# A routed mixture of experts behind an attention block on one Trainium2 core: eight blocks' P2 and P4 held back to the end of the last group

## The chip, the cores and the metric

The kernel runs on one core of one Trainium2 chip. The metric is device time in microseconds for one execution, taken as the median of several; lower is better. A profiled execution also gives the span from the first to the last instruction, the granted TensorE clock and one record for every instruction. PE is TensorE (PEld its weight loads), DVE is VectorE, ACT is ScalarE, POOL is GpSimd, SP is SyncE, which here only issues DMAs.

## The reference

An attention block with sketched features gives x with N = 4352 rows and 128 columns. Its second half routes x through eight experts:

```
logits = x @ w_gate
P = np.exp(logits - logits.max())
for _ in range(8):
    P /= P.sum(1, keepdims=True) + 1e-09
    P /= P.sum(0, keepdims=True) + 1e-09
    P *= N / E
for e in range(E):
    h = np.maximum(x @ w1[e], 0.0)      # 1024 columns
    out += P[:, e:e + 1] * (h @ w2[e])
```

All data is float32. The eight experts' two products for all rows are nearly all of the work. The routing weights are not negative, so P may be multiplied into x ahead of the ReLU.

## The kernel before

**Groups and blocks.** Rows stand transposed in `xT` (128 features by 4352 rows). They are cut into groups (line 529). Groups of two tiles come first with experts 0 and 1, without weights, while attention and routing still run; their sums are kept in `kept`. Then come five groups of three tiles with weighted rows, and at the end one last group: rows 0 to 511 as two tiles of 256, experts 2 to 7. Four blocks make up an expert there, 24 the group. A block is two of the eight slices of 128 hidden columns.

**The first product.** `first` (line 787) makes one step: two matmuls, one for each half of 64 columns of TensorE, into one of four PSUM banks named `a`, and a ReLU on ACT from there into `h`. A block has four steps, `h[0]` to `h[3]` (two slices by two tiles). The rows come weighted: `prepare_x` (line 569) loads the weights of expert e into `xe` by a DMA from `pT` on SP, and POOL multiplies `xT` into it. There are two `xe` buffers.

**The second product.** A 2x2 product of blocks is done with seven half-size products P1 to P7 instead of eight. They need differences of `h` (`ts`, made by DVE at lines 812, 814 and 815) and of w2 (`ws`). `seven` (line 870) says which product goes into which of four PSUM banks `s0` to `s3` and which half s of the 128 partitions of it (0 the lower, 1 the upper): P1 and P6 into `s0`, P2 and P4 into `s1`, P3 and P5 into `s2`, P7 into `s3`, in the half of the block's parity. Products run `LAG` = 8 steps, two blocks, behind the first product. Even blocks run half 0 ahead of half 1, odd blocks the other way, so that successive matmuls take the two halves in turn. `second` (line 921) counts products of each bank and half, and calls `part` when both halves of a bank have had their last.

**The order at the end.** `steps` issues a step of the first product, DVE's differences and the due products in turn. The order of each engine's queue comes from a scheduler; the attention and routing part fixes DVE's and PE's order by hand, the last part (lines 1060 and 1061) does not. `last_products` (line 888) gives the products of the last two blocks as P1 P6 P3 P5 P7, then P7 P1 P6 P3 P5, then the two blocks' P2 and P4. Bank `s3` completes first, then `s0`, `s2` and `s1`. `last_part` (line 660) evacuates them: ACT and DVE copy between halves of partitions, DVE adds the sums and the kept sums `k1` and `k2` of experts 0 and 1 (the two tiles of `kept[0]`) to the two results `y1` and `y2`, and `put` (line 599) transposes each and stores it in four DMAs, spread over the queues of line 751.

**The kept sums.** `weigh_kept` (line 583) loads the weights of experts 0 and 1 into `pb` by SP and lets POOL multiply both kept sums and add them. It is issued at the start of the group's fourth expert, expert 5 (line 960), behind the loads of the next expert on SP.

Of the kernel before, what the change touches and what calls it, by code (L numbers as in the profile page):

```python
# [13 lines left out]
Alu = mybir.AluOpType  # L14
# [36 lines left out]
def kernel(  # L51
# [12 lines left out]
    nc = tc.nc  # L64
# [457 lines left out]


    NMAX = 512
    NT3 = 256
# [57 lines left out]
    def weigh_kept(g):  # L583
# [6 lines left out]
        for y in ys[1:]:  # L590
            tc.keep_in_program_order(nc.gpsimd.tensor_tensor(ys[0], ys[0], y, op=Alu.add))

    lower, upper = slice(0, H2), slice(H2, P)

# [10 lines left out]
    def part(g, k):  # L605

        if groups[g][2] == 3:
            part_of_twenty(g, k)
        elif g == len(groups) - 1:
            last_part(g, k)  # L610
        else:
            part_of_seven(g, k)
# [46 lines left out]

    def last_part(g, k):  # L660

        lo, n, *_ = groups[g]
        s = sums[g][k]

        def add(out, a, b):
            nc.vector.tensor_tensor(out, a, b, op=Alu.add)

        own = parts.setdefault(g, {})
        if not own:
            own.update(y=[pools[0].tile([P, NT3], F32, name=f"y{t}", bufs=1)[:, 0:n] for t in range(2)],  # L670
                       **{a: room(a, n) for a in "zwxfr"})
        (y1, y2), z, w, x, f, r = (own[a] for a in "yzwxfr")
        k1, k2 = (kept[0][:, lo + t * n:lo + (t + 1) * n] for t in range(2))
        if k == 3:
            nc.scalar.copy(w[lower], k2[lower])
            nc.scalar.copy(r[upper], s[lower])
            add(w[upper], s[upper], r[upper])
            add(x[upper], w[upper], k1[upper])
            add(w[upper], w[upper], k2[upper])
        elif k == 0:  # L680
            nc.scalar.copy(z[lower], s[upper])
            nc.vector.tensor_copy(z[upper], s[lower])
            add(z, s, z)
            add(x[upper], x[upper], z[upper])
            add(x[lower], s[lower], k1[lower])
            add(z, z, w)
        elif k == 2:
            nc.scalar.copy(f[lower], s[upper])
            nc.scalar.copy(f[upper], s[upper])
            add(z[lower], s[lower], z[lower])  # L690
            add(y2, z, f)
            put(y2, lo + n, n, ends[1])
        else:
            add(y1, s, x)
            put(y1, lo, n, ends[0])

# [53 lines left out]

    ends = (nc.scalar, nc.sync, nc.gpsimd, nc.scalar), (nc.sync, nc.scalar, nc.gpsimd, nc.sync)

    def store(yt, b0, b1, queues):
# [13 lines left out]
    blocks = [(j, q) for j in range(len(items)) for q in range(FO // (4 if tiles_of(j) == 3 else 2))]  # L767
    LAG = 8
    hs = {}

    def room_of(k):

        lo, n, t, _, weighted = groups[items[blocks[k][0]][0]]
        if t == 3:
            if "x" not in hs:
                hs["x"] = pools[0].tile([P, 25, NT3], F32, name="hx", bufs=1)
                hs["pqg"] = pools[0].tile([P, 3, NT3], F32, name="pqg", bufs=1)
            return hs["x"] if k % 2 == 0 else hb[:, 0:25 * NT3].rearrange("p (b n) -> p b n", n=NT3)
        base = hs["x"].rearrange("p b n -> p (b n)") if weighted else hb
        size = 4 * (NT3 if weighted else 480)  # L780

        def at(i):
            return base[:, size * i:size * (i + 1)].rearrange("p (b n) -> p b n", b=4)[:, :, 0:n]

        return at(k % 3), at(3 + k % 2)

# [12 lines left out]
    def two(k):  # L799

        j, q = blocks[k]
        n = groups[items[j][0]][1]
        h, ts = hs[k] = room_of(k)

        def step(c):
            f, t = 2 * q + c // 2, c % 2
            first(k, f, t * n, (t + 1) * n, h[:, c], k % 2)

        def sums(c):

            if c == 4:
                nc.vector.tensor_tensor(ts[:, 0:2], h[:, 1::2], h[:, 0:2], op=Alu.subtract)  # L812
            elif c == 5:
                nc.vector.tensor_tensor(ts[:, 2], h[:, 3], ts[:, 0], op=Alu.subtract)  # L814
                nc.vector.tensor_tensor(ts[:, 3], h[:, 2], ts[:, 2], op=Alu.subtract)

        return 4, step, sums
# [52 lines left out]
    def seven(k):  # L870

        j, q = blocks[k]
        _, w2, ws = loaded_w[j]
        h, ts = hs[k]
        n = h.shape[2]
        lo, hi = slice(0, H2), slice(H2, DM)
        p1 = (w2[:, 2 * q, lo], h[:, 0], 0, 0, 0)
        p6 = (ws[:, 1, q], ts[:, 2], 0, 1, 0)
        p2 = (w2[:, 2 * q + 1, lo], h[:, 2], 1, 0, 0)
        p4 = (w2[:, 2 * q + 1, hi], ts[:, 3], 1, 1, 0)  # L880
        p3 = (ws[:, 3, q], h[:, 3], 2, 0, 0)
        p5 = (ws[:, 0, q], ts[:, 0], 2, 1, 0)
        p7 = (ws[:, 2, q], ts[:, 1], 3, k % 2, 0)
        if k % 2 == 0:
            return [p1, p6], [p2, p4], [p3, p5], [p7]
        return [p6, p1], [p4, p2], [p5, p3], [p7]

    def last_products(k):

        (p1, p6), (p2, p4), (p3, p5), (p7,) = seven(k)  # L890
        (r6, r1), (r4, r2), (r5, r3), (r7,) = seven(k + 1)
        ps = [(k, p) for p in (p1, p6, p3, p5, p7)] + [(k + 1, p) for p in (r7, r1, r6, r3, r5)] + [
            (k, p2), (k, p4), (k + 1, r2), (k + 1, r4)]
        return [ps[2 * i:2 * i + 2] for i in range(7)]

# [24 lines left out]

    def second(k, p):
        j, q = blocks[k]
        g, e = items[j]
        lo, n, t, es, _ = groups[g]
        w, x, i, s, place = p
        if g not in sums:
            sums[g] = [mps.tile([P, 512], F32, tag=f"s{i}", name="s")[:, 0:n * (t - 1)] for i in range(4)]
            done[g] = {}


        seen = done[g]
        c = seen[i, s] = seen.get((i, s), 0) + 1
        per = len(es) * (FO // (4 if t == 3 else 2)) * TIMES[t][i][s]
        if t == 2 and i == 3:
            per //= 2
        nc.tensor.matmul(sums[g][i][H2 * s:H2 * (s + 1), n * place:n * (place + 1)], w, x, start=c == 1,  # L936
                         stop=c == per, tile_position=(0, H2 * s))
        if c == per:
            seen[i] = seen.get(i, 0) + 1
            if seen[i] == 2:  # L940
                part(g, i)

    def steps():

        todo, sums_at, t = {}, {}, 0
        for k in range(len(blocks) + 2):
            if k == len(blocks):
                for i, ps in enumerate(last_products(k - 2)):
                    todo[t + i] = ps
            if k < len(blocks):  # L950
# [3 lines left out]
                if q == 0:  # L954
                    for i in (j, j + 1, j + 2 if j + 2 < first_weighted else j):
                        if i < len(items) and i not in sources and (pools or i < first_weighted):
                            prepare_x(i)
                        if i < len(items) and i not in loaded_w and (pools or i < first_weighted):
                            prepare_w(i)
                    if weighted and e == es[3]:  # L960
                        weigh_kept(g)
                m, step, sums_ = (four if tiles == 3 else two)(k)
                products = (twenty if tiles == 3 else seven)
# [37 lines left out]

    engines = mybir.EngineType
    with tc.manual_schedule(engines={engines.DVE, engines.PE, engines.Activation}):
# [88 lines left out]
```

## Time and profile before

| | |
|---|---|
| median of 3 timed runs | 948.29 us (947.58 to 948.32) |
| the profiled execution's own time | 947.29 us |
| its span, first to last instruction | 945.5 us |
| granted TensorE clock over the span | 0.997 |
| PE busy | 928.3 us (98%) |
| PE's weight loads busy | 548.7 us (58%) |
| DVE busy | 699.2 us (74%) |
| ACT busy | 419.2 us (44%) |
| POOL busy | 192.5 us (20%) |
| chain that ended last, by engine | PE 92%, DVE 4%, DMA 1%, issue 1% |

The profile's page sums instructions by engine and by line, cuts the span into 40 slices, and follows back the chain of work that ended last. A group of instructions shows its count, its busy time, and how long its engine stood idle before it and for whom. A timeline line reads: start, duration, engine, line, operation, output<-input, shape, count of merged instructions, and in brackets the idle time before it and who ended it. An operation and an operand's name (`hx`, `hb`: two rooms for `h` and `ts`; `s`: the banks `s0` to `s3`) tell which step it is. A matmul of the program is two records. Where stages differ, a table of stretches gives the busy time of each engine between two times.

### The profile page before, as it was taken

The page shows a single profiled execution, that of the slowest core. Times are in us where ns is not written, and L with a number is a line of the kernel's source. Part 1 is how long each engine was busy: PE and PEld are TensorE (multiplying, and loading weights), DVE is VectorE, ACT ScalarE, POOL GpSimd, SP SyncE. Part 2 cuts the span into 40 slices and gives each one's busy share as a digit, 9 for nine tenths or more (in the row PEclk, how much of TensorE's full clock was granted, in tenths as well). Part 3 has the DMA queues.
Part 4 walks back from the last instruction along what each step waited for, and adds up shares of the span by engine and source line. Part 5 has one row for each costly group of instructions (what it writes and reads, how often), then busy time and mean ns, then how long its engine had stood idle before and what let it go on. Part 6 is the DMA issues. An engine that isn't in the chain of part 4 may idle for free.

```text
span 945.5 us, 18262 instructions
## 1 busy us (share of the span) xinstructions
PE 928.3 (98%) x7162; PEld 548.7 (58%) x7162; DVE 699.2 (74%) x1215; ACT 419.2 (44%) x894; POOL 192.5 (20%) x177
## 2 busy tenths in 40 slices
PE   8999999999999999999999999999999999999996
PEld 6553535566666666665555555555555555557974
DVE  7787579987768778676886756966757977759545
ACT  2444445555444454444544444544445444445443
POOL 2000000072456511130021100201110343211120
PEclk9999999999999999999999999999999999999998
DMA  6500000212434474445353534363434555533540
GB/s 194 184 1 1 2 1 1 68 62 85 129 106 124 133 230 123 145 142 170 107 162 109 185 109 145 110 182 128 145 107 164 150 163 176 182 137 96 168 145 12
DMA packets 85863, 113.07 MB, mean 120 GB/s; under 512 B 23377, under 2 KB 67409, under 8 KB 81425
## 3 DMA queue, kind: packets, MB, share of 16 engines
q1 hardware_dynamic: 84752, 111.71, 37.6%
q8 instruction: 56, 0.92, 0.4%
q10 hardware_dynamic: 960, 0.13, 0.1%
q14 instruction: 31, 0.25, 0.1%
q0 software_dynamic: 64, 0.07, 0.0%
HBM read 99.03 MB, written 12.85 MB: 118 GB/s over the span
## 4 chain that ended last, share of the span: by engine, by line
PE 92%; DVE 4%; DMA 1%; issue 1%; POOL 0%; ACT 0%; SPq 0%; DVEq 0%; POOLq 0%; ACTq 0%
PE a L793 48%; PE s L936 41%; PE a L355 1%; PE a L377 1%; PE a L324 1%; DMA pb<-pT 1%; DMA kx<-in_k_dram 0%; DVE hb L814 0%; DVE hx L846 0%; DVE hb L812 0%; PE a L293 0%; DVE kp L309 0%; DVE qa L367 0%; DVE kT L280 0%; DVE qT L275 0%
## 5 line engine op out<-in xcount | busy, mean ns | idle before, releaser
L793 PE MATMUL a<-xe,w 128*64 128x256 f32 (+1 forms) x2560 | 517.5, 470 | 1.3 <-ACT hx L797 1.3
L797 ACT ACTIVATE hb<-a 128x256 f32<-128x256 f32 (+3 forms) x384 | 189.2, 495 | 254.3 <-PE a L793 228.5
L797 ACT ACTIVATE hx<-a 128x256 f32<-128x256 f32 (+1 forms) x368 | 170.1, 463 | 216.2 <-PE a L793 191.2
L793 PEld LDWEIGHTS a<-xe,w 128*64 128x64 f32 x2560 | 208.9, 137 | 77.4 <-ACT hx L797 1.8
L936 PE MATMUL s<-hb,ws 128*64 128x256 f32 (+2 forms) x1312 | 235.3, 400 | 0.0
L846 DVE TENSOR_TENSOR hb<-hb 128x512 f32<-128x512 f32 (+1 forms) x204 | 131.0, 652 | 101.6 <-ACT hb L797 97.3
L936 PE MATMUL s<-hx,ws 128*64 128x256 f32 x1280 | 205.0, 379 | 0.9 <-DVE kept L626 0.5
L567 POOL TENSOR_TENSOR xe<-xT,xe 128x768 f32<-128x768 f32 (+2 forms) x41 | 84.3, 2058 | 570.2 <-DMA xe<-pT 415.8
L846 DVE TENSOR_TENSOR hx<-hx 128x512 f32<-128x512 f32 (+1 forms) x204 | 151.1, 750 | 62.6 <-ACT hx L797 57.7
L936 PEld LDWEIGHTS s<-hb,ws 128*64 128x64 f32 x1312 | 108.9, 137 | 112.6 <-issue 85.3
L936 PEld LDWEIGHTS s<-hx,ws 128*64 128x64 f32 x1280 | 106.1, 137 | 98.6 <-issue 72.6
L793 PE MATMUL a<-xT,w 128*64 128x480 f32 (+2 forms) x448 | 121.9, 506 | 1.0 <-DVE xT L396 0.9
L936 PE MATMUL s<-hb,w 128*64 128x256 f32 (+2 forms) x440 | 96.7, 426 | 1.0 <-DVE kept L626 1.0
L936 PE MATMUL s<-hx,w 128*64 128x256 f32 x416 | 74.6, 379 | 0.0
L793 PEld LDWEIGHTS a<-xT,w 128*64 128x64 f32 x448 | 44.2, 137 | 32.8 <-issue 18.1
L225 POOL TENSOR_TENSOR ws<-w 128x256 f32<-128x256 f32 (+1 forms) x70 | 60.0, 892 | 13.5 <-PE a L793 11.7
L936 PEld LDWEIGHTS s<-hb,w 128*64 128x64 f32 x440 | 39.9, 137 | 27.4 <-issue 11.4
L846 DVE TENSOR_TENSOR pqg<-hb 128x512 f32<-128x512 f32 x68 | 50.8, 787 | 0.0
L936 PEld LDWEIGHTS s<-hx,w 128*64 128x64 f32 x416 | 37.8, 137 | 10.7
L812 DVE TENSOR_TENSOR hx<-hx 128x512 f32<-128x512 f32 x24 | 18.3, 761 | 30.3 <-ACT hx L797 21.6
L812 DVE TENSOR_TENSOR hb<-hb 128x960 f32<-128x960 f32 (+2 forms) x28 | 28.7, 1027 | 12.9 <-PE s L936 7.0
L846 DVE TENSOR_TENSOR pqg<-hx 128x512 f32<-128x512 f32 x68 | 35.0, 554 | 0.0
(152 smaller groups left out, 541.3 us busy)
## 6 DMA issues: line engine op xcount, KB each, us to landing
w<-in_moe_w_dram SPq DMA_DIRECT2D x82, 512.0 KB, 5.3
ws<-ws SPq DMA_DIRECT2D x34, 1024.0 KB, 4.9
xe<-pT SPq DMA_DIRECT2D x34, 384.0 KB, 3.9
ws<-ws SPq DMA_DIRECT2D x12, 512.0 KB, 4.6
pb<-pT SPq DMA_DIRECT2D x6, 384.0 KB, 6.5
kx<-in_k_dram SPq DMA_DIRECT2D x4, 544.0 KB, 4.1
qx<-in_q_dram SPq DMA_DIRECT2D x4, 544.0 KB, 5.3
v<-in_v_dram SPq DMA_DIRECT2D x32, 64.0 KB, 4.5
```

The costliest lines, as they stand in the source:

```text
L225: tc.keep_in_program_order(nc.gpsimd.tensor_tensor(ws[:, c:c + len(ns)], blocks(x), blocks(y), op=Alu.subtract if off else Alu.add))
L324: nc.tensor.matmul(pv[64 * s:64 * (s + 1), i], kp[0:n, H * t + h].rearrange("p i j -> p (i j)"), vx[0:n, slots[h], t, :], start=(t == 0 an ...
L355: nc.tensor.matmul(banks[i][m][:, 0:n], wqf[sl, m, :], qT[sl, lo:hi], start=True, stop=True, tile_position=(64 * i, 0))
L377: nc.tensor.matmul(t[64 * i:64 * (i + 1), 0:n], kvz[:, (i + m) % 2, i].rearrange("p h d -> p (h d)"), ph[i][0][:, 0:n], start=True, stop=T ...
L567: tc.keep_in_program_order(nc.gpsimd.tensor_tensor(out, x, pb, op=Alu.mult))
L793: nc.tensor.matmul(ph[sl], loaded_w[j][0][:, P * f + H2 * s:P * f + H2 * (s + 1)], sources[j][:, lo:hi], start=True, stop=True, tile_posit ...
L797: nc.scalar.activation(out=out, in_=ph, func=Act.Relu)
L812: nc.vector.tensor_tensor(ts[:, 0:2], h[:, 1::2], h[:, 0:2], op=Alu.subtract)
L846: nc.vector.tensor_tensor(out if not isinstance(out, tuple) else places(*out), places(*a), places(*b) if isinstance(b, tuple) else b, op=A ...
L936: nc.tensor.matmul(sums[g][i][H2 * s:H2 * (s + 1), n * place:n * (place + 1)], w, x, start=c == 1, stop=c == per, tile_position=(0, H2 * s))
```

## The change

The last eight blocks (experts 6 and 7) no longer run P2 and P4 where they fall due: the products are put into a list `held`, their operands `h[2]` and `ts[3]` go into a room of their own in `hb`, and both halves of the list are issued at the very end, four pairs behind the products of the last block but one, four behind those of the last. The last block's products come in another order (P7 P1, P5 P3, P6), and its differences as four DVE operations instead of three.

The kept sums are added by TensorE: `weigh_kept` is issued one expert earlier (at expert 4) and makes POOL also subtract `k2` from `k1` in the upper half; `kept_to_sums` issues four matmuls with halves of the identity at the start of expert 6, which add `k1` into both halves of `s1` and `k2` into the lower half of `s2` and the upper half of `s3`.

`last_part` is called for each half of a bank as it completes, so that copies and sums start on a half, and no longer reads `kept`. The stores of both results go on SP and ACT alone. From the last block but one on, the order of DVE, PE and ACT is the program's.

```diff
     def weigh_kept(g):
...
+        if t == 2:
+            k1, k2 = ys[0][upper, 0:n], ys[0][upper, n:2 * n]
+            tc.keep_in_program_order(nc.gpsimd.tensor_tensor(k1, k1, k2, op=Alu.subtract))
...
-    def last_part(g, k):
+    def last_part(g, k, s):
...
-        if k == 3:
-            nc.scalar.copy(w[lower], k2[lower])
-            nc.scalar.copy(r[upper], s[lower])
-            add(w[upper], s[upper], r[upper])
-            add(x[upper], w[upper], k1[upper])
-            add(w[upper], w[upper], k2[upper])
-        elif k == 0:
-            nc.scalar.copy(z[lower], s[upper])
-            nc.vector.tensor_copy(z[upper], s[lower])
-            add(z, s, z)
-            add(x[upper], x[upper], z[upper])
-            add(x[lower], s[lower], k1[lower])
-            add(z, z, w)
-        elif k == 2:
-            nc.scalar.copy(f[lower], s[upper])
-            nc.scalar.copy(f[upper], s[upper])
-            add(z[lower], s[lower], z[lower])
-            add(y2, z, f)
-            put(y2, lo + n, n, ends[1])
-        else:
-            add(y1, s, x)
-            put(y1, lo, n, ends[0])
+        if (k, s) == (3, 1):
+            nc.scalar.copy(r[upper], s3[lower])
+            add(w[upper], s3[upper], r[upper])
+        elif (k, s) == (2, 1):
+            nc.scalar.copy(f[lower], s2[upper])
+        elif (k, s) == (0, 0):
+            nc.scalar.copy(z[upper], s0[lower])
+            nc.scalar.copy(x[lower], s0[lower])
+            add(x[upper], z[upper], w[upper])
+        elif (k, s) == (2, 0):
+            add(z[upper], x[upper], s2[upper])
+            add(z[lower], s2[lower], f[lower])
+            add(z[lower], z[lower], x[lower])
+        elif (k, s) == (0, 1):
+            nc.scalar.copy(r[lower], s0[upper])
+            add(y2[upper], z[upper], s0[upper])
+            add(x[upper], x[upper], s0[upper])
+            add(y2[lower], z[lower], r[lower])
+            put(y2, lo + n, n, (nc.sync, nc.scalar))
+        elif (k, s) == (1, 1):
+            add(y1, s1, x)
+            put(y1, lo, n, (nc.sync, nc.scalar))
...
-    ends = (nc.scalar, nc.sync, nc.gpsimd, nc.scalar), (nc.sync, nc.scalar, nc.gpsimd, nc.sync)
...
+    HELD = 8
...
+        if k >= len(blocks) - HELD:
+            i = 2 * (k - len(blocks) + HELD)
+            h[2], ts[3] = hb[:, NT3 * i:NT3 * (i + 1)], hb[:, NT3 * (i + 1):NT3 * (i + 2)]
...
+        if k >= len(blocks) - HELD:
+            held.append([(k, p2), (k, p4)])
+            if k == len(blocks) - 2:
+                return [p1, p6], [p3, p5], [p7]
+            if k == len(blocks) - 1:
+                return [p7, p1], [p5, p3], [p6]
+            return ([p1, p6], [p3, p5], [], [p7]) if k % 2 == 0 else ([p6, p1], [p5, p3], [], [p7])
...
+    def last_products():
+
+        k = len(blocks) - 2
+        one, two_ = ([[(b, p) for p in ps] for ps in seven(b)] for b in (k, k + 1))
+        half = HELD // 2
+        return one + held[:half] + two_ + held[half:]
+
+    def kept_to_sums(g):
+
+        lo, n, *_ = groups[g]
+        k1, k2 = (kept[0][:, lo + t * n:lo + (t + 1) * n] for t in range(2))
+        for i, s, x in ((1, 0, k1), (1, 1, k1), (2, 0, k2), (3, 1, k2)):
+            into(g, ident[:, H2 * s:H2 * (s + 1)], x, i, s, 0)
...
-        for k in range(len(blocks) + 2):
+        for k in range(len(blocks) + 5):
+            if k == len(blocks) - 2:
+                ctx.enter_context(tc.manual_schedule(engines={engines.DVE, engines.PE, engines.Activation}))
...
-                    if weighted and e == es[3]:
+                    if weighted and e == es[3 if tiles == 3 else 2]:
                         weigh_kept(g)
+                if k == len(blocks) - HELD:
+                    kept_to_sums(g)
```

`into` is the body of `second`: it issues one product, counts it with the kept sums' matmuls, and calls `last_part` at the last one of a half.

## The prediction

> **What bounds the kernel now.** I read the page first, then the end of the span backwards: the chain of waits, the timeline by engine, and a table of stretches. TensorE is busy 928.3 of 945.5 us at a granted clock of 0.997, so a change of the last group can gain only where TensorE stands still or after it has stopped. There are two such places. The first is in the table of stretches; its columns are the stretch, its length, busy time (instructions) of PE, PEld, DVE, ACT, POOL, then clock, DMA share and GB/s.
>
> ```profile
> 889.43:895.90 6.47, 6.47 (x63) 6.46 (x61) 3.09 (x6) 3.08 (x8) 0.00 (x0) 1.00 0.31 111
> 902.38:911.48 9.10, 7.36 (x64) 6.00 (x62) 3.73 (x7) 3.41 (x10) 5.03 (x4) 1.00 0.45 152
> 917.93:924.40 6.47, 6.47 (x64) 4.30 (x62) 3.08 (x6) 3.07 (x9) 0.00 (x0) 1.00 0.04 15
> ```
>
> Each stretch runs from the start of one block's wide subtraction on DVE (L812) to that of the block two later, so each holds two blocks: 30 matmuls, each two records (a few of a neighbour fall in). Two blocks cost 6.47 us; the one around 905 costs 9.10. TensorE loses 9.10 - 6.47 = **2.63 us** there. ACT's timeline tells why:
>
> ```profile
> 904.19 0.38 ACT L797 ACTIVATE hx<-a 128x256 f32<-128x256 f32 x1 [0.47 <-PE a L793]
> 908.51 0.40 ACT L675 COPY w<-kept 64x256 f32<-64x256 f32 x1 [3.94 <-POOL kept L591]
> 908.82 1.57 ACT L797 ACTIVATE hx<-a 128x256 f32<-128x256 f32 x5
> ```
>
> A copy that the end needs (L675) was placed 30 us early in ACT's queue, waits 3.94 us for POOL's weighed sums, and holds up every ReLU behind it; TensorE fills its four banks and stops. POOL is late because its pb came late:
>
> ```profile
> 898.88 0.33 SPq L182 DMA_DIRECT2D ws<-ws  x1
> 899.25 1.02 SPq L563 DMA_DIRECT2D pb<-pT  x2
> ```
> ```profile
> 896.16 1.57 POOL L567 TENSOR_TENSOR xe<-xT,xe 128x512 f32<-128x512 f32 x1 [11.38 <-DMA xe<-pT]
> 904.64 2.50 POOL L567 TENSOR_TENSOR kept<-kept,pb 128x512 f32<-128x512 f32 x2 [6.91 <-DMA pb<-pT]
> 907.21 1.26 POOL L591 TENSOR_TENSOR kept<-kept,kept 128x512 f32<-128x512 f32 x1
> ```
>
> The second place is the end: TensorE's last products, then DVE's sums, then the stores.
>
> ```profile
> 933.22 0.38 PE L936 MATMUL s<-hx,ws 128*64 128x256 f32 x1
> 933.23 0.38 PE L936 MATMUL s<-hx,w 128*64 128x256 f32 x1
> ...
> 935.84 1.24 PE L936 MATMUL s<-hx,w 128*64 128x256 f32 x7
> ```
> ```profile
> 935.75 0.43 DVE L666 TENSOR_TENSOR w<-s,r 64x256 f32<-64x256 f32 x1 [0.22 <-ACT r L676]
> ...
> 939.69 0.42 DVE L666 TENSOR_TENSOR y<-z,f 128x256 f32<-128x256 f32 x1
> 940.15 0.77 DVE L602 STREAM_TRANSPOSE yt<-y 128x256 f32<-128x256 f32 x2
> 940.62 1.52 SPq L759 DMA_DIRECT2D out_dram<-yt  x3
> 940.63 1.40 ACTq L759 DMA_DIRECT2D out_dram<-yt  x3
> 940.92 1.33 POOL L759 DMA_DIRECT2D out_dram<-yt  x2 [30.82 <-DVE yt L602]
> ```
>
> TensorE ends at 937.08, DVE at 940.92 (940.15 + 0.77): DVE's chain, not TensorE, releases the stores.
>
> **Unit.** 30 matmuls in 6.47 us on two column halves are 15 pairs of 0.431 us: a slot. A matmul pairs when its neighbour in the order uses the other half. In the order to which both kernels are built, nothing before the last group changes on any engine.
>
> **1. The early copy goes: -2.63 us.** L675 disappears, and nothing on ACT or DVE reads kept any more. TensorE now does: four matmuls at the head of expert 6. Behind them in its queue stands all its work, so kept must be there in time. The pb loads move 13 us forward on SP, before xe of expert 6 (issued 892.08, since it waits for its buffer) and behind ws of expert 5 (issued 885.93), so to 886.3. With the 5.3 us of the chain's pb step they land at 891.6. POOL then takes 2.50 + 1.26 and the new 64x256 subtraction, 0.7 by the 0.73 of its 128x256 rows: 896.1, or 897 with DVE in between. Expert 6 begins at about 904.9 without the stall: 8 us of cover. Beyond it each us is a us. xe of expert 6, behind them on POOL, is ready at 898.6 instead of 897.7, 6 us early. xe of expert 7 keeps its time on SP, because it waits for a buffer, not for pb.
>
> **2. What the move meets: +0.2 us.** POOL's old 4 us fell where ACT stood and DVE had nothing to do. At 891.6 DVE is working. The row to read is DVE's L814 at 896.63: 1.38 us, ending 0.28 after POOL's xe, against 0.42 for L815 right behind it. The Trainium skill (SBUF — State Buffer, "SBUF: two separate sides") speaks against the move: VectorE, in an op with two SBUF inputs, and GpSimd hold a shared port pair exclusively, whoever starts first, for the whole instruction. If POOL kept it for its train of 4.4 us, DVE's sum for p6 would come at about 897, where the product wants it at 895.5: +1.5. But in the timeline at 756 to 761 (POOL's sums of weights at 1.18, 1.18 and 1.06 instead of 0.73; DVE's at 1.22 and 2.35 for two instead of 0.69 each) they take turns. If they alternate, each POOL op holding the port about 1.15 and each DVE op 0.3 (256 columns) or 0.55 (512), POOL's five ops (train and xe) from 891.65 let L814 end at 894.9 (wanted 895.5), L815 at 896.3 (wanted 896.4), and the next block's L814, behind xe, at 898.9 (wanted 898.8). I take the row: 0.2; ends 0 and 1.5.
>
> **3. Kept sums on TensorE: +0.86 us.** Four matmuls, halves 0,1,0,1, between a product on half 1 and a first matmul on half 0: two slots. Ends 0.86 and 1.7 if they run alone.
>
> **4. Held products.** Eight pairs (P2, P4) leave the blocks; two were already at the end. So the last first-matmul ends 6 x 0.431 = 2.59 us earlier. The end grows: 15 matmuls there (7.5 slots) become 27, 14 on one half and 13 on the other. Walking the order in which they are issued (last block but one: P7 of the block before it, P1, P6, P3, P5, P7; eight held; then P7, P1, P5, P3, P6 of the last; eight held), P7 of the even block pairs with the P5 before it, and no slot is lost but the last half: 14 slots, 6.04 us. Blocks without the pair take 13 matmuls, 2.80 us, where ACT has 1.54 of work and DVE 1.54 (half of 3.08), both covered; P6 is wanted 5.6 us after its block's start, its sum is ready at 4.4. Held h and differences go to hb, which no other block of this group uses.
>
> **5. The end, from T0 = start of the first slot after the last first-matmul.** T0 is 933.22 now and becomes 933.22 - 2.63 + 0.2 + 0.86 - 2.59 = **929.06**. P7 and P1 of the last block end with slot 8, T0 + 3.45 (their differences are ready at about 1.8, so today's 0.16 us wait of P7 for its difference goes). ACT's copy starts 0.24 later, as now (935.11 to 935.35), at 3.69; its four others follow at 0.38: 4.07, 4.45, 4.83, 5.21. DVE starts 0.40 after the copy's start, as now: 4.09. Its 11 sums and transposes follow at today's spacing, 0.45 where one needs the one before, 0.34 where not: 4.54, 4.99, 5.33 (its f is ready at 5.25), 5.78, 6.12, 6.45, 6.79, transpose 7.24, y1's sum 7.58, transpose 8.03, end 8.45. TensorE stops at 6.04, 1.5 before DVE asks for P2 and P4: the held products hide most of the chain. Halving operations saves nothing by itself (64x256 at 0.42, 128x256 at 0.41); that 11 of DVE's 13 operations remain, and that they start under TensorE, does. DVE ends at 929.06 + 8.45 = 937.5 against 940.92: **-3.4 us**. Ends of this part: +0.5 if ACT's copies space at 0.46, -0.3 if DVE's pairs overlap more.
>
> **6. Stores: 0.** Eight stores on SP and ACT, four each, instead of 3, 3 and 2 on POOL. The skill (DMA: Bandwidth & Descriptors, "Issuing engines are not separate DMA queues") says that several issuers save only the issue time. By that rule alone, losing one costs an issue, 0.45 to 0.68 by SP's starts (940.62, 941.3, 941.75). By the rows, POOL's issues take 0.59 to 0.75 and land 2.7 after, SP's 1.7, ACT's 2.0. With y2 ready at T0 + 7.66 and four issues 0.54 apart, the last starts at 9.3, 0.9 after DVE's end (now 0.8), and lands 1.7 to 2.0 later, about where it lands now (packets stop 2.8 after DVE's end). From there to the end of the span nothing changes. Ends: -0.4, +0.6.
>
> **Sum.** 945.5 - 3.4 = 942.1 of span; the profiled execution's 947.29 becomes 943.9. It lies 1.0 under the median of the timed runs, 948.29, which becomes **944.9 us**.
>
> **Rivals.** (a) *Only the stall goes.* If the held products don't pair (eight hb matmuls in a row, each alone), the 16 take 16 slots instead of 8 and cost up to 3.4 us at the end; -3.4 + 3.4 = no change, about 948. Against it: P2, P4, P2, P4 end the kernel now and ran seven records in 1.24 us, paired. (b) *The ports.* The full 1.5 of point 2 (1.3 more), ACT's 0.5 and the stores' 0.6 leave 3.4 - 2.4 = 1.0 gained: 947.3, within what a measurement can tell from no change (0.2%, 1.9 us). (c) *Slower: TensorE waits for kept.* The four matmuls stand at the queue's head; if pb lands d us later than 891.6, TensorE waits d - 8. From d = 13.3 (8 of cover, 3.4 of gain, 1.9) it is slower: 950.2 and up. For it: pb sits behind two weight loads that wait for TensorE. Against: those went out at 884.28 and 885.93 unhindered. (d) *More:* no port cost, stores at -0.4, sums at -0.3: 3.4 + 0.9 = 4.3, 944.0.
>
> **How the numbers follow.** Forecast 62%, (d) 18%, (a) 5%, (b) 11%, (c) 4%. The unknown costs alone give 944.0 to 946.5 for the likeliest; with a little on both sides for the timed runs' spread (0.7) the range is 943.4 to 946.7. Faster by over 0.2%: forecast, (d) and part of (b), 0.86; within: 0.09; slower: 0.05.
>
> **What would show it.** No ACT copy from kept and two blocks at 6.47 around 905 (1); DVE's L814 and L815 stretched near 892 to 899, PE without a gap (2); four s<-kept records' pairs in 0.86 (3); two blocks at 5.6 in the last 25 us and an end of 6.04 after the last first-matmul (4); DVE's last transpose 2.4 us after TensorE's end, not 3.8 (5); 4.6 us from DVE's end to the end of the span (6). A wait of TensorE on POOL at expert 6, or held matmuls one per 0.43 us, would prove it wrong.

## The result, and the profile after

The changed kernel takes **945.26 us** (median of 6 runs, 944.07 to 945.53), the kernel before 947.95 us on the same chip (6 runs, 947.58 to 948.32). The ratio is 0.997, with a 95% interval of 0.9957 to 0.9982: faster by 2.7 us where 3.4 were forecast. The profiled execution took 945.29 us, with a span of 943.5 us at a granted clock of 0.998.

The table of stretches of the changed kernel, cut from one wide subtraction on DVE to another: the last four blocks that keep all their products (13.62 us), the two blocks in which the kept sums are added, and two blocks without P2 and P4. The columns are those of the prediction.

```profile
889.67:903.29 13.62, 13.29 (x125) 10.41 (x122) 10.43 (x13) 6.17 (x17) 6.69 (x5) 1.00 0.58 179
903.29:910.62 7.33, 7.33 (x72) 4.88 (x70) 3.09 (x7) 3.06 (x9) 0.93 (x1) 1.00 0.35 115
916.66:922.27 5.61, 5.61 (x56) 3.73 (x54) 3.08 (x6) 3.06 (x9) 0.00 (x0) 1.00 0.10 40
```

The stretch of 9.10 us has gone. The kept sums cost 7.33 - 6.47 = 0.86 us and two held blocks take 5.61, both as forecast. But the four blocks ahead of them, 12.95 before (889.43 to 902.38), take 13.62. In the timelines of POOL, DVE and PE the cause stands next to it:

```profile
892.68 2.95 POOL L569 TENSOR_TENSOR kept<-kept,pb 128x512 f32<-128x512 f32 x2 [7.66 <-DMA pb<-pT]
895.71 1.33 POOL L593 TENSOR_TENSOR kept<-kept,kept 128x512 f32<-128x512 f32 x1
897.12 0.80 POOL L596 TENSOR_TENSOR kept<-kept 64x256 f32<-64x256 f32 x1
```
```profile
889.67 1.61 DVE L817 TENSOR_TENSOR hx<-hx 128x512 f32<-128x512 f32 x3 [1.75 <-PE a L800]
892.77 1.72 DVE L817 TENSOR_TENSOR hx<-hx 128x512 f32<-128x512 f32 x1 [1.50 <-ACT hx L804]
894.53 1.38 DVE L817 TENSOR_TENSOR hx<-hx 128x256 f32<-128x256 f32 x1
```
```profile
897.38 0.65 PE L967 MATMUL s<-hx,w 128*64 128x256 f32 x4 [0.33 <-DVE hx L817]
```

In the kernel before, DVE's first two differences at this place were:

```profile
892.53 0.69 DVE L812 TENSOR_TENSOR hx<-hx 128x512 f32<-128x512 f32 x1 [1.49 <-ACT hx L797]
893.26 0.42 DVE L814 TENSOR_TENSOR hx<-hx 128x256 f32<-128x256 f32 x1
```

Three differences take 1.61 us in all where POOL rests. Beside POOL's train the first takes 1.72 instead of 0.69 and the second 1.38 instead of 0.42, and TensorE stands 0.33 us for `hx`.

The timeline of the end, changed kernel:

```profile
933.26 0.60 PE L967 MATMUL s<-hx,ws 128*64 128x256 f32 x2
933.46 0.36 ACT L676 COPY r<-s 64x256 f32<-64x256 f32 x1 [3.00 <-PE s L967]
933.73 0.36 ACT L681 COPY z<-s 64x256 f32<-64x256 f32 x1
...
934.12 0.37 ACT L682 COPY x<-s 64x256 f32<-64x256 f32 x1
...
934.50 0.37 ACT L679 COPY f<-s 64x256 f32<-64x256 f32 x1
934.93 0.65 PE L967 MATMUL s<-hx,ws 128*64 128x256 f32 x4 [1.07 <-ACT f L679]
935.41 1.90 PE L967 MATMUL s<-hb,w 128*64 128x256 f32 x16
935.61 0.42 DVE L668 TENSOR_TENSOR z<-x,s 64x256 f32<-64x256 f32 x1 [0.80 <-PE s L967]
...
938.20 0.45 DVE L605 STREAM_TRANSPOSE yt<-y 128x256 f32<-128x256 f32 x1
938.67 1.52 SPq L758 DMA_DIRECT2D out_dram<-yt  x3
...
938.67 0.42 DVE L668 TENSOR_TENSOR y<-s,x 128x256 f32<-128x256 f32 x1
939.13 0.45 DVE L605 STREAM_TRANSPOSE yt<-y 128x256 f32<-128x256 f32 x1
```

The line to read is that at 934.93: P3 and what follows waits 1.07 us, and not for data. P3 adds into the lower half of `s2`; ACT's copy `f` reads the upper half, and comes as the fourth of four copies. After it DVE's sum from `s2` waits 0.80 us for P3. DVE ends at 939.58 and the span 3.9 us later, where before it was 4.6.

**Where the time went.** T0 is, as in the prediction, the start of the first slot after the last first-matmul; it is 929.80 here.

| from 945.5 to 943.5 us of span | forecast | measured |
|---|---|---|
| upstream of these stretches (889.43 became 889.67) | 0 | +0.24 |
| stall behind the early copy | -2.63 | -2.63 |
| DVE beside POOL's train (13.62 - 12.95) | +0.2 | +0.67 |
| kept sums on TensorE | +0.86 | +0.86 |
| six pairs held back, up to T0 | -2.59 | -2.56 |
| T0 to DVE's end: 7.70 before, 8.45 forecast, 939.58 - 929.80 = 9.78 | +0.75 | +2.08 |
| DVE's end to the end of the span (4.58, 3.92) | 0 | -0.66 |
| sum | -3.4 | -2.0 |

The sum is the 2.0 that the spans differ by; the term of the held pairs is what T0 leaves for them once the others are taken off. The upstream 0.24 is there from about 500 us on (the same weight load is issued at 510.74 before and at 510.98 after), where the two kernels run the same instructions: executions of one kernel differ by that much and more, so below stretches are compared rather than spans.

### The profile page after: what moved, and what is told of

It is laid out like the page before. It is cut to its first block, busy times and chain, and to the rows that moved or that the text cites. A ratio compares the mean times of both kernels' runs of the same rounds, so it can differ in the third digit from the quotient of the medians.

```text
span 943.5 us, 18269 instructions
## 1 busy us (share of the span) xinstructions
PE 929.0 (98%) x7170; PEld 545.7 (58%) x7170; DVE 704.2 (75%) x1214; ACT 419.0 (44%) x894; POOL 192.0 (20%) x176
## 4 chain that ended last, share of the span: by engine, by line
PE 93%; DVE 5%; issue 1%; ACT 0%; DMA 0%; SPq 0%; DVEq 0%; ACTq 0%
PE a L800 48%; PE s L967 41%; PE a L355 1%; PE a L377 1%; DVE hb L817 1%; PE a L324 1%; DVE hx L817 0%; DMA kx<-in_k_dram 0%; DVE hx L862 0%; PE a L293 0%; DVE qa L367 0%; DVE kT L280 0%; DVE qT L275 0%; PE a L402 0%; DVE rd L394 0%
## 5 line engine op out<-in xcount | busy, mean ns | idle before, releaser
L804 ACT ACTIVATE hb<-a 128x256 f32<-128x256 f32 (+3 forms) x392 | 191.9, 492 | 257.8 <-PE a L800 233.6
L804 ACT ACTIVATE hx<-a 128x256 f32<-128x256 f32 (+1 forms) x360 | 167.2, 465 | 213.5 <-PE a L800 190.1
L967 PE MATMUL s<-hb,w 128*64 128x256 f32 (+2 forms) x472 | 100.5, 423 | 1.0 <-DVE kept L627 1.0
L817 DVE TENSOR_TENSOR hb<-hb 128x480 f32<-128x480 f32 (+5 forms) x84 | 66.2, 790 | 14.2 <-PE s L967 6.9
L967 PE MATMUL s<-hx,w 128*64 128x256 f32 x384 | 68.3, 380 | 0.3 <-DVE hx L817 0.3
L967 PEld LDWEIGHTS s<-hb,w 128*64 128x64 f32 x472 | 42.2, 137 | 28.5 <-issue 11.4
L817 DVE TENSOR_TENSOR hx<-hx 128x256 f32<-128x256 f32 (+1 forms) x65 | 39.7, 616 | 24.5 <-ACT hx L804 19.9
L967 PEld LDWEIGHTS s<-hx,w 128*64 128x64 f32 x384 | 34.2, 137 | 10.7 <-DVE hx L817 0.8
```

The source lines that it names most:

```text
L804: nc.scalar.activation(out=out, in_=ph, func=Act.Relu)
L817: nc.vector.tensor_tensor(out, a, b, op=Alu.subtract)
```

## The experiments

Theory after the result: the stall, the kept sums and the held pairs did what the sum says; what is missing was lost in two places, DVE beside POOL, and the two halves of a bank, which two engines never use at once in this program. Rivals: the loss beside POOL has another cause; the end is limited by DVE's chain alone; the shorter rest of the span comes from POOL's missing stores. The table lists all runs; each but the one named is the changed kernel with an edit. "Four blocks" is the stretch that took 12.95 before, "chain" is T0 to DVE's end, "rest" from there to the end of the span.

| | time (runs), us | before beside it | ratio, 95% interval | span | four blocks | chain | rest |
|---|---|---|---|---|---|---|---|
| the change | 945.26 (6) | 947.95 | 0.9957 to 0.9982 | 943.5 | 13.62 | 9.78 | 3.9 |
| 1 copies behind P6 | 944.91 (5) | 948.11 | 0.9953 to 0.9979 | 943.1 | 13.27 | 9.65 | 3.8 |
| 2 no POOL sums | 944.62 (1) | 948.11 | | 942.8 | 12.95 | 9.77 | 3.9 |
| 3 three queues | 944.99 (1) | 948.11 | | 943.2 | 12.95 | 9.77 | 3.9 |
| 4 only the order (on the kernel before) | 946.10 (10) | 948.11 | 0.9968 to 0.9987 | 944.4 | 13.52 | 8.36 | 4.4 |
| 5 kept sums late | 952.03 (1) | 947.73 | | 950.2 | 12.93 | 9.50 | 3.9 |
| 6 banks in turn | 944.36 (1) | 947.73 | | 942.6 | 12.96 | 9.15 | 3.9 |
| 7 and two held pairs first | 943.55 (4) | 947.73 | 0.9941 to 0.9975 | 941.8 | 13.58 | 8.27 | 3.9 |
| 8 and the kept sums spread | 943.25 (5) | 947.52 | 0.9938 to 0.9965 | 941.8 | 12.95 | 8.28 | 3.8 |
| 9 two blocks held | 946.69 (1) | 947.73 | | 944.9 | 13.62 | 8.48 | 3.8 |
| 10 transposes together | 946.94 (1) | 947.71 | | 945.2 | 13.42 | 9.49 | 4.5 |
| 11 as 8, one held pair first | 942.74 (4) | 947.71 | 0.9929 to 0.9963 | 941.4 | 12.95 | 7.84 | 3.8 |

**1. The copies and sums called behind the last P6.**

```diff
-                last_part(g, i, s)
+                due.append((g, i, s))
+                if (i, s) in ((0, 1), (1, 0), (1, 1)):
+                    while due:
+                        last_part(*due.pop(0))
```

> The changed kernel, but the copies and sums on half banks of the last block are issued in the program only after its P6, so that none of them stands between two products of one bank. Theory: in the changed kernel TensorE's 1.07 us gap before P3 is a wait for ACT's copy f, which reads the other half of P3's bank; dependencies are kept by bank. Then the gap goes: from the first slot after the last first-matmul (T0) TensorE ends at about +6.3 instead of +7.5, and DVE ends at +8.9 instead of +9.8 (ACT's copy z now waits for P6, as both stand in bank s0, 0.5 later than I had forecast), so the span is 0.9 us shorter than the changed kernel's, about 942.6. Rival: P3 waits for the ReLU of its own h[3]; then the gap stays at 1.1 and DVE ends at +9.8.

TensorE's gap is gone, as expected: it ends at 935.84, 6.2 us after T0 (forecast 6.04, with the gap 7.5). DVE's end came only 0.13 closer to T0, not 0.9. The timeline shows the end of TensorE and why DVE gained so little:

```profile
933.74 2.10 PE L967 MATMUL s<-hb,w 128*64 128x256 f32 x15
934.55 0.42 DVE L668 TENSOR_TENSOR x<-z,w 64x256 f32<-64x256 f32 x1 [0.44 <-ACT z L681]
935.32 0.42 DVE L668 TENSOR_TENSOR z<-x,s 64x256 f32<-64x256 f32 x1 [0.35 <-ACT f L679]
```

DVE too waits for ACT's copies, the second time for `f`, which reads the bank that the sum reads. So the theory was half of it: each of PE, ACT and DVE is held by another's access to the bank, and taking TensorE's wait away moved that sum, on `s2`, only from T0 + 5.81 to T0 + 5.68.

**2. POOL's sums left out.** The diff takes POOL's two multiplies, add and subtraction from the last group; the loads of `pb` stay.

> The changed kernel without POOL's four operations on the kept sums (they go into the result unweighted and without expert 1's); the pb loads stay. Theory: the 0.68 us that the four blocks around 889.67 to 903.29 lost in the changed kernel (13.62 instead of 12.94) is DVE kept off its port by POOL's train; then the four blocks take 12.94 and TensorE waits nowhere. Rival: the pb loads or a weight load are late there; then 13.6 stays.

```profile
889.68:902.63 12.95, 12.95 (x123) 12.27 (x121) 7.13 (x13) 6.14 (x16) 1.59 (x1) 1.00 0.64 187
```

The stretch of the changed kernel's 13.62 takes 12.95, TensorE is busy throughout, and DVE's three differences beside the loads take 1.61 us:

```profile
892.76 1.61 DVE L819 TENSOR_TENSOR hx<-hx 128x512 f32<-128x512 f32 x3 [1.48 <-ACT hx L806]
```

So it is POOL's operations that stretch the differences, not the moved loads. The 12.95 alone would not show it, since the next run reaches it with POOL's operations in place.

**3. The stores on three queues**, as they were before the change:

```diff
-            put(y2, lo + n, n, (nc.sync, nc.scalar))
+            put(y2, lo + n, n, (nc.sync, nc.scalar, nc.gpsimd, nc.sync))
...
-            put(y1, lo, n, (nc.sync, nc.scalar))
+            put(y1, lo, n, (nc.scalar, nc.sync, nc.gpsimd, nc.scalar))
```

> The changed kernel with the stores of the two results on SP, ACT and POOL as before the change (3, 3 and 2). From DVE's end to the end of the span it took 4.58 us before and 3.92 after. Theory: the 0.66 us come from POOL's two stores, which land last or have to be drained; then 4.5 to 4.6 comes back. Rival: they come from the earlier start of the first result's stores (DVE ends the two transposes 0.9 apart now, 0.35 before); then 3.7 to 3.9 stays.

The rest of the span stays at 3.9 us: POOL's stores cost nothing that shows, and their theory falls. A by-product was more useful. POOL's train ran here just as in the changed kernel, yet the four blocks took 12.95:

```profile
887.02 0.90 SPq L565 DMA_DIRECT2D pb<-pT  x2
892.35 2.94 POOL L569 TENSOR_TENSOR kept<-kept,pb 128x512 f32<-128x512 f32 x2 [6.88 <-DMA pb<-pT]
```
```profile
893.22 0.95 DVE L817 TENSOR_TENSOR hx<-hx 128x512 f32<-128x512 f32 x1 [1.48 <-ACT hx L804]
```

POOL began 0.87 us ahead of DVE's wide subtraction, against 0.09 in the changed kernel (892.68, 892.77). All runs that kept the train can be put in one row:

| run | change | 1 | 3 | 6 | 7 | 9 | 10 |
|---|---|---|---|---|---|---|---|
| POOL's start ahead of DVE's | 0.09 | 0.41 | 0.87 | 0.73 | 0.12 | 0.07 | 0.29 |
| loss, four blocks less 12.95 | 0.67 | 0.32 | 0.00 | 0.01 | 0.63 | 0.67 | 0.47 |
| sum | 0.76 | 0.73 | 0.87 | 0.74 | 0.75 | 0.74 | 0.76 |

Where there is a loss, loss and lead make up 0.75: `hx` comes a fixed time after POOL's start, and how late that is depends on when `pb` landed. It landed, with POOL's start taken for it, 5.33 us after its issue in run 3 and 6.12 after it in the changed kernel:

```profile
886.56 0.90 SPq L565 DMA_DIRECT2D pb<-pT  x2
```

Over the seven runs it took 5.33 to 6.13, behind the same weight load, so the 0.67 is that of the profiled execution; others of the same kernel may lose less. This row was found afterwards, in runs made for other ends; no run moved the landing alone.

**4. One edit to the kernel before:** its last blocks' order on DVE, PE and ACT is made the program's, which alone keeps the copy L675 from being placed early.

```diff
+            if k == len(blocks) - 2:
+                ctx.enter_context(tc.manual_schedule(engines={engines.DVE, engines.PE, engines.Activation}))
```

> The kernel before, with one edit: from the last block but one the order of ACT, DVE and PE is the program's, so ACT's copy from kept stands at the end instead of 30 us ahead. No block is held, the kept sums are still DVE's. Theory: the stall around 905 was this copy alone; two blocks there take 6.47 instead of 9.10 and the time falls by about 2.6 us (0.28%), as much as the whole change brought, so the rest of the change sums to nothing. Rival: TensorE would have waited there for something else late (a weight load, xe of expert 6): then 1 us or more of the 2.6 stays, and the held products are worth the remainder.

It is faster, 0.9977 (0.9968 to 0.9987), by 2.0 us. The stall of 2.63 is gone, but POOL's operations, which used to fall where DVE had nothing to do, now stand beside DVE (its wide subtraction takes 1.65 us at 905.91), and four blocks take 13.52. The end in the program's order costs 8.36 - 7.70 = 0.66. So the order alone gives 2.0 us where the whole change gives 2.7; the two intervals overlap, so that these times cannot tell the two kernels apart, and what the rest of the change is worth has to be read from the stretches (run 9). In both places where the train of POOL stood it met DVE.

**5. The kept sums weighed one expert later**, in their old place (`e == es[3]`), while TensorE still adds them at expert 6.

> The changed kernel with the kept sums weighed at expert 5, as before the change, instead of at expert 4. This is the place of my rival (c): four matmuls on kept stand at the head of TensorE's queue at expert 6. pb then lands near 904.6 and POOL's four operations, beside DVE's, end near 910; TensorE comes for them near 905.1. Theory: it stands 4.5 to 5 us there, the loss near 895 moves here and is covered, and the span becomes 943.5 + 4 to 5, about 948, slower than the kernel before. Rival: TensorE works on what it has and loses under 1 us.

PE's timeline and the table of stretches of this run:

```profile
904.95 0.59 PE L967 MATMUL s<-hx,ws 128*64 128x256 f32 x2
910.10 1.98 PE L967 MATMUL s<-kept,ident 128*64 128x256 f32 x8 [4.56 <-POOL kept L596]
911.87 1.07 PE L800 MATMUL a<-xe,w 128*64 128x256 f32 x4
```
```profile
905.54:910.10 4.56, 0.00 (x0) 0.00 (x0) 3.71 (x3) 0.12 (x1) 4.35 (x4) 0.80 0.51 172
910.10:915.00 4.90, 4.90 (x24) 2.82 (x26) 0.00 (x0) 0.64 (x2) 1.26 (x1) 0.50 0.00 0
915.00:918.00 3.00, 3.00 (x30) 1.92 (x28) 0.75 (x2) 1.28 (x4) 0.00 (x0) 0.98 0.00 0
```

The same place in the changed kernel:

```profile
905.63 0.38 PE L967 MATMUL s<-hx,ws 128*64 128x256 f32 x1
905.64 0.38 PE L967 MATMUL s<-kept,ident 128*64 128x256 f32 x1
```

The wait of 4.56 us is as large as expected. The span is 6.7 us longer than the change's, not 4 to 5, and T0 comes 7.0 later (936.80). Three terms make this up. The gap between records understates the pause: in the changed kernel the first matmul on `kept` runs beside the product ahead of it, so here it would have started at 904.95 and comes 5.15 late. After the pause the granted clock is 0.50 for 4.9 us; 24 matmul records, at 6.47 / 60 us each at full clock, are 2.6 us of work, so 2.3 us more are lost there, and from the first matmul on `kept` to T0 it is 26.70 us against 24.16, 2.54 more. The four blocks ahead won 0.69, since the train had left them: 5.15 + 2.54 - 0.69 = 7.0. This is the prediction's slower rival, at work once its cover is taken away.

**6. The banks in turn:** P6 is put ahead of P3 and P5, and ACT's copies follow behind the products, so that a bank is read when TensorE has left it.

```diff
-                return [p7, p1], [p5, p3], [p6]
+                return [p7, p1], [p6, p3], [p5]
...
-                last_part(g, i, s)
+                due.append((g, i, s))
+                if (i, s) == (2, 1):
+                    for i_, s_ in ((3, 1), (2, 1), (0, 0), (2, 0), (0, 1)):
+                        last_part(g, i_, s_)
+                elif i == 1:
+                    last_part(g, i, s)
```

> The changed kernel with another order at the end: the last block's products as P7 P1 P6 P3 P5, so that a bank's two halves follow each other; ACT's copies as r, z, f, x, r, all issued behind the products. Theory: what set the end is that two engines never touch the two halves of one bank at once: in the run with the copies behind P6 TensorE no longer waited, but DVE's first sum on bank s2 still waited for ACT's fourth copy f on that bank and started at T0 + 5.68 (T0 + 5.81 in the changed kernel, 4.99 in my prediction). With f third it starts at T0 + 5.0, DVE ends at T0 + 8.5 instead of 9.8, the span is about 942.3. Rival: the end is set by DVE's own dependent sums or by TensorE's held products; then DVE still ends at +9.6 or later.

```profile
934.59 0.42 DVE L668 TENSOR_TENSOR z<-x,s 64x256 f32<-64x256 f32 x1
...
938.18 0.45 DVE L605 STREAM_TRANSPOSE yt<-y 128x256 f32<-128x256 f32 x1
```

TensorE has no gap, and the timeline shows no wait of DVE behind its first sum. The sum on `s2` starts at T0 + 5.11 (T0 is 929.48), close to the 5.0 expected, where it was 5.81 in the changed kernel: the order of the banks was worth 0.70. The chain falls from 9.78 to 9.15, half of the 1.3 expected, because from that sum to its end DVE needs 4.04 us. The expectation, like the prediction, had counted about 3.5; the changed kernel needs 3.97.

**7. And two held pairs ahead of the last block's products instead of four** (`half = HELD // 4`).

> The same as the run with the banks in turn, but only two of the eight held pairs stand ahead of the last block's products and six behind, instead of four and four. Theory: DVE's chain starts two slots (0.86 us) earlier and TensorE still ends before y1's sum asks for it (T0 + 6.3 against + 6.7); DVE ends at T0 + 7.6, the span is 0.86 shorter than with four and four, about 941.5. Rival: TensorE's end or the last block's differences (ready at T0 + 1.8) set the time and nothing or less than 0.4 us is gained.

The chain starts and ends 0.88 earlier than in run 6, as expected. Its end, at T0 + 8.27, is not the T0 + 7.6 expected, since run 6 had come out 0.65 later than the value that this was counted from.

**8. And POOL's work on the kept sums spread:** loads and multiplies at the group's second expert (expert 3), the add at expert 4, the subtraction at expert 5. The expectation calls them the third, fourth and fifth.

```diff
+        if e == 3:
+            for i, y in enumerate((y0, y1)):
+                weigh(y, y, weights_of(i, lo, 2 * n, "pb"))
+        elif e == 4:
+            tc.keep_in_program_order(nc.gpsimd.tensor_tensor(y0, y0, y1, op=Alu.add))
+        elif e == 5:
+            tc.keep_in_program_order(nc.gpsimd.tensor_tensor(y0[upper, 0:n], y0[upper, 0:n], y0[upper, n:2 * n],
+                                                             op=Alu.subtract))
```

> The kernel with the banks in turn and two held pairs ahead, and beside it GpSimd's work on the kept sums spread: the loads of the weights and the two multiplies come with the third expert of the last group's order, the add with the fourth, the subtraction with the fifth, where they stood in one train before. Theory (the 0.5 to 0.7 us lost around 893 to 903 are DVE kept from its turn by a train of four GpSimd operations, so that hx comes late once): with one or two of them to an expert the 0.33 us gap of TensorE goes, the last four gated blocks take 12.94 to 13.1 us instead of 13.5, and the span is 0.4 to 0.5 us below 941.8, at about 941.3; the median is about 943.1. Rival (the loss depends on the operations' sum, not on their standing in a train, or the earlier loads of the weights collide with the gathers and weight loads there): no gain or a loss of up to 0.5 us, median 943.5 to 944.

```profile
890.29:903.24 12.95, 12.95 (x123) 12.47 (x121) 7.54 (x12) 6.15 (x16) 2.53 (x2) 1.00 0.48 147
```

The four blocks take 12.95 and TensorE's gap is gone. The span did not fall, because this execution came to the group 0.79 us later than that of run 7 (a weight load issued at 859.75 there and at 860.54 here, the same lag as at about 510 us); its T0 is 0.16 later, so the edit won about 0.6 in between. The medians, 4.18 and 4.27 us under the kernel before, cannot tell the two apart.

**9. Two blocks held instead of eight** (`HELD = 2`, on the changed kernel).

> The changed kernel with two held blocks instead of eight (one pair ahead of the last block's products, one behind; the kept sums' four matmuls at the last block but one). Theory: the held products are worth what they hide of the chain: T0 comes 2.6 us later, DVE's chain starts 1.3 us earlier from it, so DVE ends 1.3 us later and the span is about 944.8. Rival: they hide nothing; then the span stays at 943.5.

The span is 944.9, 0.1 from what was expected. From the start of the four blocks (889.93 here, 889.67 in the changed kernel) to DVE's end it takes 1.3 us longer: T0 comes 2.6 us later and the chain is 1.3 shorter. That is what holding eight blocks rather than two is worth. No run moves the kept sums to TensorE by itself; their cost of 0.86 us is measured, what they save on DVE is not set apart.

**10. The transposes together:** on the changed kernel, y2's `put` moves behind y1's sum.

```diff
             add(y2[lower], z[lower], r[lower])
-            put(y2, lo + n, n, (nc.sync, nc.scalar))
         elif (k, s) == (1, 1):
             add(y1, s1, x)
+            put(y2, lo + n, n, (nc.sync, nc.scalar))
             put(y1, lo, n, (nc.sync, nc.scalar))
```

> The changed kernel with one move: the transpose and the stores of y2 stand behind the sum of y1, so that the two transposes of DVE run 0.35 us apart at the end, as they did before the change, instead of 0.93. Stores on the two queues of the changed kernel. Theory (the 0.66 us that the stretch from DVE's end to the end of the span lost come from the earlier start of y2's stores, which leaves fewer issues behind the last transpose): DVE ends at about the same place or 0.1 earlier, 939.5, and the rest of the span is 4.4 to 4.7 us instead of 3.92; the span is about 944.0 to 944.2. Rival (POOL's queue or something else makes the difference): the rest stays at 3.9 and the span at 943.4 to 943.5.

```profile
939.59 0.42 DVE L668 TENSOR_TENSOR y<-s,x 128x256 f32<-128x256 f32 x1
939.93 0.76 DVE L605 STREAM_TRANSPOSE yt<-y 128x256 f32<-128x256 f32 x2
```

The rest of the span rises from 3.9 to 4.5 us, the chain falls by 0.29. So the rest is shorter when the first four stores leave earlier, and the net gain of the spread transposes is 0.3 us or a little less. The span itself, 945.2, missed: this execution came to the last group 1.6 us late, over the same instructions.

**11. As 8, one held pair ahead** (`half = HELD // 8`).

> The kernel with the kept sums spread, the banks in turn, and now one held pair ahead of the last block's products instead of two, seven behind. Theory (what is left of the end is DVE's chain, which starts with the last block's P7; TensorE is done 2.07 us before DVE and has that much to give): P7 comes one slot, 0.43 us, earlier, DVE's first sum at 2.75 us after T0 instead of 3.18, and DVE's end at T0 + 7.85 instead of 8.27; the span is about 941.4 and the median 942.8. Rival (P7 waits for its difference, which DVE makes about 1.8 us after T0, or the copies and sums queue behind each other): TensorE shows a gap of up to 0.4 us at the first products of the last block and the span stays at 941.8.

```profile
932.54 0.43 DVE L681 TENSOR_TENSOR w<-s,r 64x256 f32<-64x256 f32 x1 [0.91 <-ACT r L689]
...
937.19 0.45 DVE L618 STREAM_TRANSPOSE yt<-y 128x256 f32<-128x256 f32 x1
```

DVE's first sum comes 2.75 us after T0 and its end 7.84, as expected; no gap of TensorE. At 942.74 us, 0.9946 of the kernel before (0.9929 to 0.9963), this is the lowest median of all: 5.0 us under the kernel before beside it, where the change is 2.7 under its own. Its interval overlaps those of runs 7 and 8, so that only the chain tells it from them.

## Why the prediction came out as it did

The time forecast was 944.9 and is 945.26; the mechanism was right, and three terms of the sum were mis-sized, partly against each other. That the time comes so close is in part luck: the kernel before took 947.95 beside the change, 0.34 less than the 948.29 counted from, and a gain of 0.66 that no step foresaw covers half of the 1.33 that step 5 missed. The profiled gain is 2.0 us where 3.4 were counted.

- **Step 1, the stall: right.** The wait at the copy is gone and with it 2.63 us; run 4 gets most of that by order alone. The 8 us of cover for `kept` were 7.7: POOL's subtraction ends at 897.92, and the first of the kept matmuls starts at 905.64.
- **Step 2, "+0.2": 0.67.** The term that failed is the landing of `pb`. The step let POOL start at 891.65, 5.3 us after the issue, which is 0.9 ahead of DVE's wide subtraction (892.53 before), and said that taking turns would then cost almost nothing. Run 3 has just this, landing after 5.33 and a loss of 0.00. In the changed kernel `pb` took 6.12 and POOL started 0.09 ahead. The model by turns held: it had L814 and L815 end 3.25 and 4.65 us after POOL's start, and the differences in their place end 3.23 and 4.64 after it (895.91 and 897.32). P4's difference, the second, was wanted at 896.4, which is 896.64 with the upstream 0.24: it comes 0.68 late, and that is the loss. The rule of the Trainium skill (SBUF — State Buffer, "SBUF: two separate sides"), by which the engine that starts first keeps the other out for its whole instruction, fits these rows: the wide subtraction takes 1.72 beside a POOL operation of 1.27. It speaks of one instruction, not of a train, and DVE's next operation does start inside the train, at 894.53, and not behind it at 897.9. The upper end of 1.5 us was too high.
- **Step 3, kept sums "+0.86", and step 4, held pairs "2.59 earlier": right**; the stretches give 0.86 and 2.56. Run 9 puts the worth of holding eight blocks rather than two at 1.3 us.
- **Step 4's end, "14 slots, 6.04 us": 7.5.** The slots pair as walked; 1.07 us of the rest is the wait of P3 for ACT. Without it run 1 ends at 6.2.
- **Step 5, "T0 + 8.45": 9.78.** This is the step that failed, in two terms. The first is the bank. The step took DVE's start from ACT's and walked DVE's own operations, but had nothing for a bank of which one half is written while the other is read. The copy `f` stood fourth in ACT's queue, P3 behind it, and DVE's sum on `s2` behind P3: it starts at T0 + 5.81 where 4.99 was counted, 0.82 late. Run 1 shows that the wait of TensorE alone is not it; run 6, with the banks in turn, has that sum at 5.11. The second is DVE's own spacing: from that sum to the end the step counted 3.46 us, and it takes 3.97 here and 4.04 in run 6, where the timeline shows no wait of DVE. Five of DVE's operations were counted at 0.34 after the one before, as not needing it; four of them came at 0.44 to 0.47. Why they do stays open. The ends of this part (-0.3, +0.5) did not reach that far. Of the bank, the Trainium skill (PSUM — Partial Sum Buffer, "PSUM bank collisions raise a hardware error") says that different quarters of a bank's partitions may be accessed at the same time and that a guard by the whole bank is the simple version; this program waits by the bank, which cost the 1.07. No run here tried the finer guard.
- **Step 6, stores "0": -0.66.** The step compared the queues, and run 3 shows that these make no difference. It had moved y2's transpose ahead of y1's sum in step 5, where that lengthens DVE's chain, and did not take the earlier issue of four stores off the rest. Run 10 puts both back.
- **The rivals.** (a), held products that do not pair, is refuted by the 16 records in 1.90 us at 935.41. (b), the ports, came with 0.67 of its 1.5 us, and of (d) only the stores came. (c), TensorE waiting for `kept`, did not come about; run 5 made it happen.

## What to carry to other kernels

An operation that waits at the head of a queue holds up all that stands behind it (2.63 us here; the order alone, run 4, won 2.0): before splitting products and sums, look for the one early instruction that stalls an engine, and fix its order. Where a result is taken from a bank by halves, write down for each bank which engine touches it in which order; two halves are not two buffers as long as the program's waits go by the bank. A train of GpSimd operations beside VectorE cost from 0 to 0.67 us here, by where it started, so spread it, or start it well before the operation that matters.

## What the runs showed of the hardware

In run 5 a TensorE that stood for 4.56 us came back at half its clock (0.50) for the next 4.9 us, and the time from there to T0 grew by 2.54 us beyond the pause, where the prediction's rival (c) took each us of waiting for one us. In finer slices of that trace the clock is 1.00 until 908.0, 0.81 from there to 908.5, and 0.50 until about 915.1: it fell 2.5 to 3.0 us after the last record ahead of the pause had ended (905.54), and was back some 6.6 to 7.1 us later. The Trainium skill (TensorE: Matmul & The Clock Gate, "Part 1: The HAM clock gate (the "warmup" mystery)") states such a fall after at least one idle window of about 3.4 us, and a return after at least one window of sustained work, with windows that run on whatever the kernel does. Two windows would be 6.8 us, an estimate from that page's figure, and the run's time at half clock agrees with it; the fall came somewhat sooner than a whole idle window. The stops of 1.07 and 0.33 us in the changed kernel left the granted clock at 1.00 in the stretches around them.
